# A scan and a segmented attention in one kernel: a new memory plan, crossbar transposes, row-wise attention outputs and big weights as the stationary operand

## The chip, the cores and the metric

The kernel runs on one core of one Trainium2 chip. The metric is the device time of one execution in microseconds (us), lower is better; the kernel before takes 1421 us. Times are medians of several executions.

Names: PE is TensorE (matmul), PEld its weight loads, DVE is VectorE, ACT is ScalarE, POOL is GpSimd, SP is SyncE, which here mostly issues DMAs. SBUF is the on-chip memory, PSUM the matmul accumulators, HBM the memory off the core. Of a matmul's two operands, one is loaded first and stays (the stationary one, loaded by PEld), the other streams past it (the moving one). "Crossbar" stands for DMAs that transpose on the way (DMA_TRANSPOSE in the traces); `xbar` in the code is something else, the mean of B's x.

## The reference, cut to what matters

Two independent halves are computed and set side by side in the output.

```python
# A: a complex diagonal scan. L = 2048 rows, 1024 channels in, 1024 states
Lam_bar = exp(dt * Lam);  Bu = x @ B_bar.T              # complex: two real matmuls
for t in range(L):
    h = Lam_bar * h + Bu[:, t]                           # the scan
y = 2.0 * real(hseq @ Cmat.T) + x * Dskip

# B: 64 segments of 32 rows, 8 memory rows before each; 32 heads of 128
mem = mem0
for s in range(64):
    h = concat([mem, x[:, 32*s : 32*s+32]])              # 40 rows
    q, k, v = h @ Wq, h @ Wk, h @ Wv
    p = softmax(where(mask, q @ k.T * 128**-0.5, -1e9))
    o = (p @ v) @ Wo
    mem = o[:, :8]                                       # next segment's memory
    outs.append(o[:, 8:])
out = concat([y, concat(outs)], axis=-1)                 # bf16, 2048 x 2048
```

B looks serial, because each segment needs the memory rows of the one before. Both kernels **guess** these rows (mean of the segment's 40 rows, with the unknown memory rows taken as zero, times Wv, times Wo), run all segments at once, **check** at the end that the computed memory agrees with the guess, and would fall back on a serial loop if it did not.

## The kernel before: the parts that matter here

Four stages follow each other. (1) *Scan stage*: A's input matmuls and scan, with B's value projection between them. (2) *Scan output and guess*. (3) *Attention*, with the q and k projections between its units. (4) *Out-projection and check*.

Inputs arrive row by row and are needed with the contraction dimension on the partitions, so PE transposes them through PSUM, 128 columns at a time. This is A's x; B's x, and A's input and output weights, are done alike:

```python
        for t in range(4 * tb, 4 * tb + 4):
            xn = self.stg.tile([128, D], BF16, name="a_stg")
            k.SP.dma_start(xn[:], self.x[0][t * 128:(t + 1) * 128, :])
            pt = k.ps("P", (128, 1024), BF16)
            for c in range(KC):
                k.PE.transpose(pt[:, c * 128:(c + 1) * 128], xn[:, c * 128:(c + 1) * 128], k.ident[:])
            k.copy("s" if t % 2 else "v", self.xT[:, :, t * 128:(t + 1) * 128], ...)
```

The scan states go to HBM at the end of every scan unit and come back in the next stage:

```python
        k.SP.dma_start(self.hs[tb][:, pc, :, :], h[:])          # stage1, 32 times
        ...
        hl = pool.tile([128, PC, 2, TB], BF16, name="a_hl", bufs=2)
        k.SP.dma_start(hl[:], self.hs[tb][:])                   # stage2, 4 times
```

An attention unit covers two groups of 99 rows (three segments each) of two heads. Scores stand with the keys on the partitions, so the sum over keys is a matmul with ones; ACT makes its reciprocal as exp(-ln):

```python
        PE.matmul(sm[:, 0:W4], k.ones[0:GW, :], mf, start=True, stop=True)      # 396 wide
        k.S.activation(ln[:], sm[:, 0:W4], ACT.Ln)
        k.S.activation(r[:]..., ln[:], ACT.Exp, scale=-1.0, accum_out=...)
        for gg in range(2):
            for hh in range(2):
                PE.matmul(o[:, gg, hh, :], vt[:, 2 * u + gg, hh * 128:(hh + 1) * 128], m[:, gg, hh, :], ...)
        V.tensor_tensor(ot[...], o[:, :, :, 0:GX], r[:, :, :, 0:GX], ALU.mult)
```

The guess (`og`, then `guess`) has a small stationary operand of 64 or 73 columns and streams the 512-wide weights past it. Its results then stand the wrong way round and are transposed. The check works the same way.

```python
        for c in range(KC):                                                     # og
            k.PE.matmul(p[0:NSEG, :], self.xbar[:, c, :], w[:, c, :], ...)
        ... copy, 4 transposes, copy
```

At the start of the attention stage the program does this:

```python
            wo0 = t32.tile([128, H, 512], BF16, name="t32")
            b.load_wqk(0)
            b.v_mem(0)                                # value rows of the memory, needs 1 MB of Wv
            ...
            k.SP.dma_start(wo0[:], b.Wo[:, :, 0:512]) # 4 MB, first needed in the last stage
```

Of the kernel before, what the change touches and what calls it, by code (L numbers as in the profile page):

```python
# [38 lines left out]
XE = T + NM  # L39

# [6 lines left out]
class K:  # L47
    def __init__(self, tc, ctx):
        self.tc, self.nc = tc, tc.nc
        nc = tc.nc  # L50
        self.V, self.G, self.S, self.PE, self.SP = nc.vector, nc.gpsimd, nc.scalar, nc.tensor, nc.sync
        self.cst = ctx.enter_context(tc.tile_pool(name="cst", bufs=1, side="left"))
        self.psp = ctx.enter_context(tc.tile_pool(name="ps", bufs=1, space=PSUM))
        self.drp = ctx.enter_context(tc.tile_pool(name="dr", bufs=1, space=DRAM))

    def ps(self, tag, shape=(128, 512), dt=FP32):
        return self.psp.tile(list(shape), dt, name="ps" + tag, bufs={"P": 3, "S": 2, "R": 1, "O": 2}[tag])
# [8 lines left out]
def consts(k):  # L66
# [6 lines left out]
    k.ones = c.tile([128, 128], BF16, name="ones")  # L73
    V.memset(k.ones[:], 1.0)

    k.segs = c.tile([128, 4], BF16, name="segs")
    V.memset(k.segs[:], 0.0)
    for j in range(4):
        V.memset(k.segs[32 * j:32 * j + 32, j:j + 1], 1.0)
    k.hpb = c.tile([128, 1], FP32, name="hpb")  # L80
    V.memset(k.hpb[:], HALF_PI)

# [42 lines left out]

class PartA:
    def __init__(self, k, x, Lre, Lim, Bre, Bim, Cre, Cim, logdt, Dskip, out):
        self.k = k
        self.x, self.Lre, self.Lim, self.Bre, self.Bim = x, Lre, Lim, Bre, Bim
        self.Cre, self.Cim, self.logdt, self.Dskip, self.out = Cre, Cim, logdt, Dskip, out  # L130
        self.hs = [k.drp.tile([128, PC, 2, TB], BF16, name=f"a_hs{i}") for i in range(NB)]

    def params(self, pool, tmp):
        k = self.k; V, S, PE, nc = k.V, k.S, k.PE, k.nc
        r24 = tmp.tile([3 * PC, 128], BF16, name="a_r24")
        for i, src in enumerate((self.Lre, self.Lim, self.logdt)):
            nc.scalar.dma_start(r24[i * PC:(i + 1) * PC, :], src.rearrange("(c p) -> c p", p=128))
        pr = k.ps("R")
        PE.matmul(pr[:, 0:3 * PC], r24[:], k.ident[0:3 * PC, 0:3 * PC], start=True, stop=True)
        raw = pool.tile([128, 3, PC], FP32, name="a_raw")  # L140
# [3 lines left out]
        def small(name):  # L144
            return pool.tile([128, PC], FP32, name=name)
        dtb = pool.tile([128, PC], BF16, name="a_dtb")
# [28 lines left out]
        self.rr, self.turn, self.bre, self.bim = rr, turn, bre, bim  # L175
        self.jf = pool.tile([128, TB + 1], FP32, name="a_jf")
        ji = tmp.tile([128, TB + 1], I32, name="a_k1")
# [24 lines left out]

    def load_x(self, tb):
        k = self.k
        for t in range(4 * tb, 4 * tb + 4):
            xn = self.stg.tile([128, D], BF16, name="a_stg")
            k.SP.dma_start(xn[:], self.x[0][t * 128:(t + 1) * 128, :])
            pt = k.ps("P", (128, 1024), BF16)
            for c in range(KC):
                k.PE.transpose(pt[:, c * 128:(c + 1) * 128], xn[:, c * 128:(c + 1) * 128], k.ident[:])  # L210
            k.copy("s" if t % 2 else "v", self.xT[:, :, t * 128:(t + 1) * 128], pt[:].rearrange("p (c n) -> p c n", c=KC))

    def load_b(self, pc):
        k = self.k
        self.bt = self.btp.tile([128, 2, KC, 128], BF16, name="a_bt")
        for i, w in enumerate((self.Bre, self.Bim)):
            wn = self.stg.tile([128, D], BF16, name="a_stg")
            k.SP.dma_start(wn[:], w[pc * 128:(pc + 1) * 128, :])
            pt = k.ps("R", (128, 1024), BF16)
            for c in range(KC):  # L220
                k.PE.transpose(pt[:, c * 128:(c + 1) * 128], wn[:, c * 128:(c + 1) * 128], k.ident[:])
            k.copy("s", self.bt[:, i, :, :].rearrange("p c n -> p (c n)"), pt[:])

    def load_c(self, blk):

        k = self.k
        for i, w in enumerate((self.Cre, self.Cim)):
            wn = self.stg.tile([128, D], BF16, name="a_stg")
            k.SP.dma_start(wn[:], w[blk * 128:(blk + 1) * 128, :])
            pt = k.ps("R", (128, 1024), BF16)  # L230
            for c in range(PC):
                k.PE.transpose(pt[:, c * 128:(c + 1) * 128], wn[:, c * 128:(c + 1) * 128], k.ident[:])
            k.S.activation(self.CT[:, i, :, blk * 128:(blk + 1) * 128], pt[:].rearrange("p (c n) -> p c n", c=PC),
                           ACT.Copy, scale=(-1.0 if i == 1 else 1.0))

    def stage1(self, pc, tb):
# [4 lines left out]
        ur = k.ps("S"); ui = k.ps("O")  # L241
        for i, u in enumerate((ur, ui)):
            for c in range(KC):
                PE.matmul(u[:], self.bt[:, i, c, :], self.xT[:, c, tb * TB:(tb + 1) * TB], start=(c == 0), stop=(c == KC - 1))  # L244
# [3 lines left out]
        V.tensor_tensor(wr[:], ur[:], c_, ALU.mult)  # L248
        V.tensor_tensor(ta[:], ui[:], s_, ALU.mult)
        V.tensor_tensor(wr[:], wr[:], ta[:], ALU.add)  # L250
        V.tensor_tensor(wi[:], ui[:], c_, ALU.mult)
        V.tensor_tensor(ta[:], ur[:], s_, ALU.mult)
# [15 lines left out]
        h = self.wp.tile([128, 2, TB], BF16, name="a_h")  # L268
# [3 lines left out]
        V.tensor_tensor(h[:, 0, :], n1[:], n2[:], ALU.subtract)  # L272
        V.tensor_tensor(n1[:], gr[:], ts2[:], ALU.mult)
        V.tensor_tensor(n2[:], gi[:], tc2[:], ALU.mult)
        V.tensor_tensor(h[:, 1, :], n1[:], n2[:], ALU.add)
        k.SP.dma_start(self.hs[tb][:, pc, :, :], h[:])

    def stage2(self, pool):

        k = self.k; V, G, PE = k.V, k.G, k.PE  # L280
        dB = pool.tile([128, D], BF16, name="a_dB")
        k.SP.dma_start(dB[:], self.Dskip.unsqueeze(0).to_broadcast([128, D]))
        for tb in range(NB):
            hl = pool.tile([128, PC, 2, TB], BF16, name="a_hl", bufs=2)
            k.SP.dma_start(hl[:], self.hs[tb][:])
            for tt in range(4):
                t0 = tb * TB + tt * 128
                xn = pool.tile([128, D], BF16, name="a_xn2", bufs=2)
                k.SP.dma_start(xn[:], self.x[0][t0:t0 + 128, :])
                xd = pool.tile([128, D], FP32, name="a_xd", bufs=2)  # L290
                G.tensor_tensor(xd[:], xn[:], dB[:], ALU.mult)
                ot = pool.tile([128, D], BF16, name="a_ot", bufs=2)
                for half in range(2):
                    hs = slice(half * 512, (half + 1) * 512)
                    py = k.ps("O")
                    for pc in range(PC):
                        for i in range(2):
                            PE.matmul(py[:], hl[:, pc, i, tt * 128:(tt + 1) * 128], self.CT[:, i, pc, hs],  # L298
                                      start=(pc == 0 and i == 0), stop=(pc == PC - 1 and i == 1))
                    V.tensor_tensor(ot[:, hs], py[:], xd[:, hs], ALU.add)  # L300
                    yield
                k.SP.dma_start(self.out[0, t0:t0 + 128, 0:D], ot[:])



class PartB:
    def __init__(self, k, x, mem0, Wq, Wk, Wv, Wo, out):
# [6 lines left out]
        self.os = [k.drp.tile([128, 8, T], BF16, name=f"b_os{i}") for i in range(4)]  # L314
        c = k.cst
        self.m0T = c.tile([128, KC, M], BF16, name="b_m0T")
        self.omT = c.tile([128, H, NM], BF16, name="b_omT")
        self.gm = c.tile([NM, D], FP32, name="b_gm")
# [3 lines left out]
        self.accR = c.tile([128, HP * NU], FP32, name="b_accR")  # L322
# [3 lines left out]
    def init(self, tmp):  # L326
        k = self.k
        k.V.memset(self.accE[:], 0.0)
        m0 = tmp.tile([M, D], BF16, name="b_m0", bufs=1)
        k.nc.scalar.dma_start(m0[:], self.mem0[0])  # L330
        pm = k.ps("R")
        for c in range(KC):
            k.PE.matmul(pm[:, c * M:(c + 1) * M], m0[:, c * 128:(c + 1) * 128], k.ident[0:M, 0:M], start=True, stop=True)
# [4 lines left out]
        z = tmp.tile([32, 512], BF16, name="b_zero", bufs=1)  # L338
        k.V.memset(z[:], 0.0)
        for hb in range(HB):  # L340
            k.G.dma_start(self.vx[hb][64 + NMX:GX, :], z[0:GX - 64 - NMX, :])
            k.G.dma_start(self.vx[hb][T + 32:NSLOT, :], z[0:32, :])

    def load_x(self, t):
        k = self.k
        if t == 0:
            self.pbar = k.ps("P")
        pbar = self.pbar
        xn = self.stg.tile([128, D], BF16, name="b_stg", bufs=3)
        k.nc.scalar.dma_start(xn[:], self.x[0][t * 128:(t + 1) * 128, :])  # L350
        pt = k.ps("P", (128, 1024), BF16)
        for c in range(KC):
            k.PE.transpose(pt[:, c * 128:(c + 1) * 128], xn[:, c * 128:(c + 1) * 128], k.ident[:])
            k.PE.matmul(pbar[:, c * NSEG + 4 * t:c * NSEG + 4 * t + 4], xn[:, c * 128:(c + 1) * 128], k.segs[:], start=True, stop=True)
        ptv = pt[:].rearrange("p (c n) -> p c n", c=KC)
        if t == 0 or t == TT - 1:
            a = XMAIN if t == 0 else t * 128 - 64
            k.copy("s", self.xe[:, :, a:a + 64], ptv[:, :, 0:64])
            b = 0 if t == 0 else T - 64
            k.copy("s", self.xe[:, :, b:b + 64], ptv[:, :, 64:128])  # L360
        else:
            k.copy("s", self.xe[:, :, t * 128 - 64:t * 128 + 64], ptv)

    def fin_xbar(self, tmp):
        k = self.k
        pb = self.pbar[:].rearrange("p (c s) -> p c s", c=KC)
        ms = tmp.tile([128, KC], FP32, name="b_ms", bufs=1)
# [577 lines left out]
```

## Time and profile before

| stage | from, to (us) | PE busy | what limits it |
|---|---|---|---|
| scan stage | 0 to 433 | 395 us | PE; waits for x at the start |
| scan output and guess | 433 to 571 | 129 us | PE |
| hole | 571 to 592 | 0.3 us | a weight load |
| attention | 592 to 1158 | 566 us | PE |
| drain | 1158 to 1176 | 9 us | ACT for the last units, then a wait for the out-projection's input |
| out-projection, check | 1176 to 1420 | 236 us | PE |

The first lines are from the page of the kernel before: busy time by engine, then 40 equal slices of the span, each digit a busy share in tenths.

```profile
span 1420.3 us, 20776 instructions
PE 1335.1 (94%) x8087; PEld 697.2 (49%) x8162; DVE 665.4 (47%) x1495; ACT 488.7 (34%) x1203; POOL 208.0 (15%) x283
...
PE   4889999999997999499999999999999988999998
DMA  5343333243328631943434343433333236213000
...
HBM read 112.50 MB, written 49.30 MB: 114 GB/s over the span
```

PE is the bound nearly everywhere. Next are the same engines' busy times by stretch. The columns are: stretch, its length, busy time and count of PE, PEld, DVE, ACT and POOL, then PE's granted clock (1.00 is full), the DMA engines' share and GB/s.

```profile
0.00:35.00 35.00, 16.45 (x156) 11.70 (x159) 18.97 (x62) 16.46 (x24) 19.22 (x87) 1.00 0.57 187
35.00:100.00 65.00, 54.31 (x440) 32.68 (x445) 39.80 (x80) 33.83 (x46) 0.00 (x0) 0.87 0.42 134
100.00:433.00 333.00, 324.02 (x1642) 151.94 (x1674) 266.54 (x509) 141.40 (x226) 0.00 (x0) 1.00 0.33 108
433.00:571.00 138.00, 129.08 (x578) 59.08 (x589) 24.94 (x41) 3.01 (x4) 33.95 (x16) 0.96 0.51 183
571.00:592.00 21.00, 0.27 (x1) 0.14 (x1) 0.93 (x13) 0.00 (x0) 0.00 (x0) 0.56 1.04 337
592.00:1158.00 566.00, 566.00 (x4137) 328.68 (x4136) 292.38 (x740) 268.41 (x835) 147.25 (x171) 1.00 0.35 100
1158.00:1176.00 18.00, 8.60 (x76) 5.20 (x75) 8.04 (x27) 13.28 (x46) 7.54 (x10) 0.66 1.03 329
1176.00:1420.00 244.00, 236.36 (x1067) 107.81 (x1087) 13.84 (x27) 12.37 (x24) 0.00 (x0) 0.98 0.22 71
```

In attention PE is busy in every microsecond of 566, while DVE and ACT are near half. PE stands still in the hole, for half of the drain, and for 29 us of the first 100. PE's waits, longest first (what waited, for whom: us in total, times, longest):

```profile
PE psP L451 <- DMA b_wv<-in_B_Wv_dram: 21.2, 1, 21.2
PE psP L210 <- DMA a_stg<-in_A_x_dram: 18.2, 6, 9.8
PE psP L615 <- DMA b_ol<-b_os_96: 5.4, 1, 5.4
...
PE psO L298 <- DMA a_hl<-a_hs_76: 3.7, 1, 3.7
PE psS L428 <- DMA b_wog<-in_B_Wo_dram: 3.3, 1, 3.3
```

Two groups of instructions of an attention unit, the sum matmul and the logarithm that follows (busy us in all, mean ns of one, idle time before). The matmul's mean is its whole passage; one follows the other after 0.167 us in a stream:

```profile
L546 PE MATMUL psR<-b_m,ones 99*128 99x396 bf16 x176 | 59.4, 337 | 3.9 <-POOL b_m L537 3.0 <-ACT b_ln L550 0.8
...
L550 ACT ACTIVATE b_ln<-psR 128x396 f32<-128x396 f32 x176 | 87.1, 495 | 0.0
```

### The profile page before, as it was taken

What the parts mean: (1) busy time and instruction counts of PE and PEld (TensorE: products, weight loads), DVE (VectorE), ACT (ScalarE), POOL (GpSimd) and SP (SyncE); (2) the same over time, 40 slices, a digit from 0 to 9 for tenths busy, and PEclk for the clock granted to TensorE, in tenths of its full rate; (3) what the DMA queues carried; (4) which work ended last, traced back from release to release, by engine and by line L of the source; (5) the groups of instructions that cost most, each with busy time, mean ns of one, the idle gap of its engine ahead of it and who ended that gap; (6) DMA issues with size and microseconds to landing.
All of it is one profiled execution on the core that took longest, in us unless ns stands there. A gap on an engine that the chain in (4) does not pass through costs nothing. (4 is left out here: it accounts for less than half of the span.)

```text
span 1420.3 us, 20776 instructions
## 1 busy us (share of the span) xinstructions
PE 1335.1 (94%) x8087; PEld 697.2 (49%) x8162; DVE 665.4 (47%) x1495; ACT 488.7 (34%) x1203; POOL 208.0 (15%) x283
## 2 busy tenths in 40 slices
PE   4889999999997999499999999999999988999998
PEld 3454444444443444255555555555555543444443
DVE  5648988787681122145555555555555550001000
ACT  4453444444431000024444444444444460000000
POOL 5000000000001222012222222222222230000000
PEclk9899999999998999699999999999999988999999
DMA  5343333243328631943434343433333236213000
GB/s 185 127 133 112 104 104 111 97 136 117 112 82 299 246 129 60 292 110 92 123 92 124 92 123 92 124 92 94 92 94 92 61 126 208 94 55 111 23 16 24
DMA packets 159742, 163.20 MB, mean 115 GB/s; under 512 B 9152, under 2 KB 132656, under 8 KB 159128
## 3 DMA queue, kind: packets, MB, share of 16 engines
q1 hardware_dynamic: 156760, 157.13, 35.2%
q10 hardware_dynamic: 2368, 4.22, 0.9%
q8 instruction: 66, 1.08, 0.3%
q0 software_dynamic: 512, 0.47, 0.1%
q14 instruction: 36, 0.29, 0.1%
HBM read 112.50 MB, written 49.30 MB: 114 GB/s over the span
## 5 line engine op out<-in xcount | busy, mean ns | idle before, releaser
L388 PE MATMUL psP<-b_wv,b_xe 128*128 128x512 bf16 x1006 | 228.2, 381 | 1.1
L507 PE MATMUL psP<-b_xe,b_wk 128*128 128x480 bf16 x1024 | 225.8, 365 | 0.0
L507 PE MATMUL psP<-b_xe,b_wq 128*128 128x480 bf16 x1024 | 223.4, 365 | 0.0
L534 ACT ACTIVATE b_e<-psS 99x396 bf16<-99x396 f32 x176 | 88.5, 503 | 374.5 <-PE psS L531 370.8
L537 POOL TENSOR_TENSOR b_m<-b_e,maskB 99x396 bf16<-99x396 bf16 x160 | 139.8, 873 | 348.8 <-ACT b_e L534 348.8
L557 DVE TENSOR_TENSOR b_ot<-psO,b_r 128x384 bf16<-128x384 f32 x176 | 98.2, 558 | 192.0 <-ACT b_r L551 178.8
L388 PEld LDWEIGHTS <-b_xe 128*128 128x128 bf16 x1024 | 99.9, 98 | 118.3 <-issue 2.4
L615 PEld LDWEIGHTS <-b_ol 128*128 128x128 bf16 x896 | 88.1, 99 | 112.9 <-DMA b_ol<-b_os_96 5.2
L507 PEld LDWEIGHTS <-b_wq 128*128 128x128 bf16 x1024 | 95.7, 97 | 93.7
L507 PEld LDWEIGHTS <-b_wk 128*128 128x128 bf16 x1024 | 95.4, 97 | 92.6
L298 PE MATMUL psO<-t_111,a_hl 128*128 128x512 bf16 x500 | 114.0, 386 | 4.4 <-DMA a_hl<-a_hs_76 3.7
L61 ACT ACTIVATE b_vst<-psP 128x512 bf16<-128x512 f32 x128 | 75.4, 589 | 95.9 <-PE psP L388 90.0
L615 PE MATMUL psP<-t_5172,b_ol 128*128 128x512 bf16 x438 | 101.5, 386 | 5.8 <-DMA b_ol<-b_os_96 5.4
L63 DVE CAST b_ost<-psP 128x512 bf16<-128x512 f32 x16 | 11.1, 692 | 200.3 <-PE psP L615 200.3
L615 PE MATMUL psP<-wo_12598,b_ol 128*128 128x512 bf16 x438 | 98.9, 379 | 0.5
L551 ACT ACTIVATE b_r<-b_ln 128x396 f32<-128x396 f32 x176 | 94.2, 535 | 5.4
L550 ACT ACTIVATE b_ln<-psR 128x396 f32<-128x396 f32 x176 | 87.1, 495 | 0.0
L61 ACT ACTIVATE b_ost<-psP 128x512 bf16<-128x512 f32 x16 | 9.6, 597 | 218.1 <-PE psP L615 204.9
L298 PEld LDWEIGHTS <-a_hl 128*128 128x128 bf16 x512 | 50.7, 99 | 66.2 <-DMA a_hl<-a_hs_76 4.2
L244 PEld LDWEIGHTS <-a_bt 128*128 128x128 bf16 x512 | 48.7, 99 | 55.7 <-issue 5.3
L300 DVE TENSOR_TENSOR a_ot<-psO,a_xd 128x512 bf16<-128x512 f32 x32 | 22.1, 692 | 110.8 <-PE psO L298 87.5
L244 PE MATMUL psS<-a_xT,a_bt 128*128 128x512 bf16 x242 | 63.8, 391 | 1.4 <-issue 1.0
(492 smaller groups left out, 1568.9 us busy)
## 6 DMA issues: line engine op xcount, KB each, us to landing
b_wv<-in_B_Wv_dram SPq DMA_DIRECT2D x16, 1024.0 KB
b_wog<-in_B_Wo_dram SPq DMA_DIRECT2D x8, 1024.0 KB
b_wq<-in_B_Wq_dram SPq DMA_DIRECT2D x16, 512.0 KB
b_wk<-in_B_Wk_dram SPq DMA_DIRECT2D x16, 512.0 KB
a_stg<-in_A_x_dram SPq DMA_DIRECT2D x16, 256.0 KB
b_stg<-in_B_x_dram ACTq DMA_DIRECT2D x16, 256.0 KB
out_dram<-a_ot SPq DMA_DIRECT2D x16, 256.0 KB
t_5172<-in_B_Wo_dram SPq DMA_DIRECT2D x1, 4096.0 KB
```

Source lines behind the costliest of these rows:

```text
L61: self.S.activation(out, in_, ACT.Copy)
L244: PE.matmul(u[:], self.bt[:, i, c, :], self.xT[:, c, tb * TB:(tb + 1) * TB], start=(c == 0), stop=(c == KC - 1))
L298: PE.matmul(py[:], hl[:, pc, i, tt * 128:(tt + 1) * 128], self.CT[:, i, pc, hs], start=(pc == 0 and i == 0), stop=(pc == PC - 1 and i == 1))
L300: V.tensor_tensor(ot[:, hs], py[:], xd[:, hs], ALU.add)
L388: k.PE.matmul(p[:], self.xe[:, c, t * 128:(t + 1) * 128], w[:, c, :], start=(c == 0), stop=(c == KC - 1))
L507: PE.matmul(p[:, 0:480], w[i][:, c, hh * 128:(hh + 1) * 128], self.xe[:, c, 480 * q:480 * q + 480], start=(c == 0), stop=(c == KC - 1))
L534: k.S.activation(e[:], s[0:GW], ACT.Exp, scale=float(E) ** -0.5, accum_out=self.accE[0:GW, i:i + 1])
L537: k.G.tensor_tensor(m[:], e[:], mask[0:GW, :, :].unsqueeze(2).to_broadcast([GW, 2, 2, GW]), ALU.mult)
L550: k.S.activation(ln[:], sm[:, 0:W4], ACT.Ln)
L551: k.S.activation(r[:].rearrange("p a b q -> p (a b q)"), ln[:], ACT.Exp, scale=-1.0, accum_out=self.accR[:, i:i + 1])
L557: V.tensor_tensor(ot[:, :, 2 * u * GX:(2 * u + 2) * GX].rearrange("p h (g n) -> p g h n", n=GX), o[:, :, :, 0:GX], r[:, :, :, 0:GX], ALU.mult)
L615: PE.matmul(p[:], lhs, self.wo[half][:, h, :], start=(h == 0), stop=(h == H - 1))
```

## The change

The intent is a new memory plan. Scan states stay in SBUF, which leaves out their way through HBM. Transposing loads go through the DMA crossbar, and PE and PSUM are spared. Attention outputs are made row-wise (queries on the partitions), so that the softmax sum is one more column of the value matmul. Guess and check take the big weights as the stationary operand. Six rotating 8 KB-per-partition buffers hold most of the weights, so the next stage's weights can be loaded ahead. Part of the out-projection is moved up to fill the drain. The core of a long diff, with cuts:

```diff
 def load_x(self, tb):                                          # A; B's x, B_re/B_im and C alike
-            xn = self.stg.tile([128, D], BF16, name="a_stg")
-            k.SP.dma_start(xn[:], self.x[0][t * 128:(t + 1) * 128, :])
-            ... 8 PE transposes and a copy
+        self.xT[tb] = k.w8((KC, TB), "xT")
+        k.SP.dma_start(self.xT[tb], self.x[0][tb * TB:(tb + 1) * TB, :], transpose=True)
 ...
-        k.SP.dma_start(self.hs[tb][:, pc, :, :], h[:])
+            self.hs[tb] = self.hsp.tile([128, PC, 2, TB], BF16, name="a_hs", bufs=4)
 ...
 def og(self, hb, w):
-        for c in range(KC):
-            k.PE.matmul(p[0:NSEG, :], self.xbar[:, c, :], w[:, c, :], ...)
-        ... copy, 4 transposes
+        for h in range(4):
+            for c in range(KC):
+                k.PE.matmul(p[:, h * NSEG:(h + 1) * NSEG], w[:, c, h * 128:(h + 1) * 128], self.xbar[:, c, :], ...)
 ...
 def att_back(self, hp, u, m):
-        PE.matmul(sm[:, 0:W4], k.ones[0:GW, :], mf, start=True, stop=True)
-        k.S.activation(ln[:], sm[:, 0:W4], ACT.Ln)
-        k.S.activation(r[:]..., ln[:], ACT.Exp, scale=-1.0, accum_out=...)
-                PE.matmul(o[:, gg, hh, :], vt[:, 2 * u + gg, hh * 128:(hh + 1) * 128], m[:, gg, hh, :], ...)
+                cs = slice(hh * 129, hh * 129 + 129)               # 128 values and a column of ones
+                PE.matmul(o[:, gg, cs], m[:, j * GW:j * GW + 128], vt[:, 2 * u + gg, cs], start=True, stop=True)
+        V.reciprocal(r..., ends)                                    # 99 x 4
+        V.tensor_tensor(ot..., oa[:, :, 1:257]..., r...to_broadcast([GW, 2, 2, E]), ALU.mult)
+            k.SP.dma_start(os[64:64 + 20 * GX, cs]..., ot[0:GX, 1:21, :])   # to HBM, rows of 512 B
 ...
 def load_o(self, tb, q):                                       # and back, transposed
+        k.SP.dma_start(t[:], self.os[q][tb * 512:(tb + 1) * 512, :], transpose=True)
 ...
-            k.SP.dma_start(wo0[:], b.Wo[:, :, 0:512])
+                if u == 4 and 8 <= hp < 12:
+                    w = k.w8((8, 512), "wo0")
+                    k.SP.dma_start(w, b.Wo[:, 8 * (hp - 8):8 * (hp - 7), 0:512])
+                if done == want:
+                    next(early, None)                               # out-projection ahead
```

## The prediction

> **What bounds the kernel now.** TensorE: the page shows PE busy 94% of 1420.3 us. Spacing in the timeline: a 128x512 matmul every 0.216 us in a stream, a 480-wide one every 0.203, a 99-wide one every 0.044, the 396-wide ones matmul 0.167. In the busy-time-by-stretch view: scan stage to 433 us, scan output and guess to 571, attention with projections 592 to 1158, its drain to 1176, out-projection to the end. DVE is 75 to 85% busy in the scan stage, under 55% in attention; the DMA engines about a third. PE falls short in five places: the first 100 us (29 us idle, clock 0.87 from 35 to 100, waits on x loads); 433 to 450 (10 us idle); 571 to 592 (21.2 us for b_wv, the longest wait); 1158 to 1176 (about 15 us: last units without projections, then 5.4 us for b_ol); the last 7 us.
>
> **What the change does.**
> 1. Crossbar DMA transposes replace 512 PE transposes (8 in 0.44 to 0.6 us) and 128 segment-sum matmuls: about -36 us of PE in the scan stage, and their ACT and DVE copies. DVE gains five segment sums (about 4 us each, estimated from 0.69 us per 512 elements).
> 2. Scan states stay in SBUF: 16.8 MB of DMA and the 3.7 us wait for a_hl vanish. Mostly off the critical path.
> 3. Attention: values become the moving operand (129 wide with a ones column), so the 396-wide sum matmul, Ln and second Exp go. Per unit PE loses 0.167 us and gains 4 x 0.013: -0.12 us x 176 = -20 us, in a PE-bound stage. ACT's cut (495 + 535 + 189 ns per unit) is off the path, except in the drain.
> 4. Stationary weights in guess, og and check: each time 64 512-wide matmuls (13.8 us) become 256 of 64 to 73. At 0.05 to 0.06 us (estimated from the transposes' spacing), 13 to 15 us: nothing won but dropped transposes and copies.
> 5. The next stage's weights are loaded ahead through six rotating buffers: the 21.2 us wait should go, and most of the 433 us gap.
> 6. Out-projection work (48 matmuls in attention, 144 right after) fills the drain: about -12 us.
> Attention outputs go to HBM in 512 B pieces and come back through the crossbar, 16 MB; hidden if it is quick.
>
> **Sum (us).** Scan stage 346 of PE + 9 first load + 20 start-up, cold clock and DVE stalls = 375; scan output and guess 127 (502); attention 566 - 20 + 10 moved in + 5 boundary = 561 (1063); tail 211 + check 14 + stalls 6 + end 7 = 238. About 1301; plus 5 for crossbar loads at the start: 1306 us, 8% less. Range 1265 to 1365.
>
> **Uncertain: crossbar speed.** No trace here has it. The Trainium skill ("Advanced Engine Details and Errata", X-Bar Transpose) says trn2 transposes run about as fast as ordinary DMA; before moved 187 GB/s in the first 35 us. The new start wants 8 MB transposed in about 65 us, 125 GB/s, plus weights. At 100 GB/s or below the start loses 25 us or more, the tail (5 MB wanted right after attention) some 15.
>
> **Signs.** Right: scan stage ends near 375; no wait over 5 us on b_wv; attention near 33.5 us per head pair with PE near 100%; no hole before the out-projection. Wrong: PE waits on b_xe, xT or b_ol transposes; PE below 95% in the scan stage because DVE (over 90%) holds psO; attention slowed by two instead of three psP buffers, or by late b_v.
>
> **What would make it wrong.** Slow crossbar DMAs, or in-order SP issue behind a blocked DMA.
>
> Chances: faster by over 2% 0.92, within 2% 0.04, slower 0.04.

## The result, and the profile after

The changed kernel takes **1281.13 us** (median of four, 1279.19 to 1283.15), the kernel before 1421.03 us (four, 1419.6 to 1422.62). The ratio is 0.9018, with a 95% interval of 0.8999 to 0.9036: 9.8% less time. Ratios here and below are from runs of the same rounds; they are not quite the ratios of the medians quoted.

The page of the changed kernel:

```profile
span 1277.1 us, 19342 instructions
PE 1236.8 (97%) x7815; PEld 650.2 (51%) x7885; DVE 630.8 (49%) x1330; ACT 320.2 (25%) x746; POOL 213.3 (17%) x307
...
PE   6698999999999999999999999999999999999997
...
HBM read 72.65 MB, written 43.66 MB: 91 GB/s over the span
```

PE lost 98 us of work and 45 us of idle time (span less PE busy: 85.2 before, 40.3 after). Its busy times by stretch, with the same columns as before:

```profile
0.00:35.00 35.00, 19.55 (x88) 8.42 (x90) 17.99 (x36) 7.13 (x12) 22.55 (x91) 1.00 1.03 207
35.00:100.00 65.00, 57.76 (x256) 25.94 (x261) 61.51 (x121) 26.39 (x46) 0.00 (x0) 0.92 0.56 140
100.00:372.00 272.00, 266.13 (x1428) 124.78 (x1452) 238.30 (x456) 99.95 (x176) 0.00 (x0) 0.99 0.34 98
372.00:492.00 120.00, 117.45 (x756) 57.67 (x769) 36.70 (x64) 3.80 (x5) 37.36 (x40) 1.00 0.57 176
492.00:1052.00 560.00, 559.44 (x4089) 330.30 (x4091) 257.77 (x620) 171.94 (x488) 153.34 (x176) 1.00 0.59 121
1052.00:1277.00 225.00, 216.43 (x1205) 103.11 (x1224) 18.50 (x37) 10.96 (x19) 0.00 (x0) 0.99 0.39 88
```

| stage | before (us) | predicted | after |
|---|---|---|---|
| scan stage | 433 | 375 | 371.8 |
| scan output and guess, with the hole | 159 | 127 | 120.0 |
| attention | 566 | 561 | 560.0 |
| drain, out-projection, check | 262 | 238 | 225.3 |

The last attention units count to the drain before and to attention after.

Attention is still PE without a gap; it lost the sum matmuls and took in out-projection work. The hole and the drain are gone. The two longest waits that PE has left lie at the start, where the DMA engines are now full (share 1.03); the third ends at 113 us, the fourth lies in the scan output stage:

```profile
PE psO L262 <- DMA w<-in_A_x_dram: 11.5, 1, 11.5
PE psP L402 <- DMA b_xe<-in_B_x_dram: 10.9, 1, 10.9
PE psS L402 <- DMA w<-in_B_Wv_dram: 4.5, 1, 4.5
PE psS L316 <- DVE a_ot L318: 1.8, 1, 1.8
```

### The profile page after: what moved, and what is told of

It reads as the page before. It is cut to its first block, busy times and chain, and to the rows that moved or that the text cites. A ratio compares the mean times of both kernels' runs of the same rounds, so it can differ in the third digit from the quotient of the medians.

```text
span 1277.1 us, 19342 instructions
## 1 busy us (share of the span) xinstructions
PE 1236.8 (97%) x7815; PEld 650.2 (51%) x7885; DVE 630.8 (49%) x1330; ACT 320.2 (25%) x746; POOL 213.3 (17%) x307
## 3 DMA queue, kind: packets, MB, share of 16 engines
q8 instruction: 63, 1.03, 0.3%
## 5 line engine op out<-in xcount | busy, mean ns | idle before, releaser
L522 PE MATMUL psP<-b_xe,w 128*128 128x480 bf16 x2048 | 439.6, 366 | 0.0
L522 PEld LDWEIGHTS <-w 128*128 128x128 bf16 x2048 | 194.2, 98 | 185.2
L77 DVE CAST b_q<-psP 128x480 bf16<-128x480 f32 (+1 forms) x192 | 98.1, 532 | 151.1 <-PE psP L522 139.6
L402 PEld LDWEIGHTS <-b_xe 128*128 128x128 bf16 x1024 | 100.8, 99 | 138.9 <-DMA b_xe<-in_B_x_dram 10.9
L622 PEld LDWEIGHTS <-b_ol 128*128 128x128 bf16 x1024 | 99.5, 98 | 117.5
L75 ACT ACTIVATE b_k<-psP 128x480 bf16<-128x480 f32 x128 | 73.3, 572 | 306.2 <-PE psP L522 306.2
L402 PE MATMUL psP<-w,b_xe 128*128 128x512 bf16 x509 | 122.4, 382 | 11.0 <-DMA b_xe<-in_B_x_dram 10.9
L262 PE MATMUL psO<-w,a_bt 128*128 128x512 bf16 x487 | 115.9, 383 | 12.8 <-DMA w<-in_A_x_dram 11.5
L402 PE MATMUL psS<-w,b_xe 128*128 128x512 bf16 x508 | 123.2, 385 | 4.8 <-DMA w<-in_B_Wv_dram 4.5
L573 DVE TENSOR_TENSOR b_ot<-psO,b_rall 99x512 bf16<-99x512 f32 x176 | 121.6, 691 | 6.4
L622 PE MATMUL psO<-b_xe,b_ol 128*128 128x512 bf16 x500 | 112.2, 379 | 0.6
L622 PE MATMUL psO<-w,b_ol 128*128 128x512 bf16 x376 | 84.4, 379 | 0.4
```

The source lines that it names most:

```text
L75: self.S.activation(out, in_, ACT.Copy)
L77: self.V.tensor_copy(out, in_)
L262: PE.matmul(u[:, i, :], self.bt[:, i, c, :], self.xT[tb][:, c, :], start=(c == 0), stop=(c == KC - 1))
L402: k.PE.matmul(p[:], self.xe[:, c, t * 128:(t + 1) * 128], w[:, c, :], start=(c == 0), stop=(c == KC - 1))
L522: PE.matmul(p[:, 0:480], w[:, i * KC + c, hh * 128:(hh + 1) * 128], self.xe[:, c, 480 * q:480 * q + 480], start=(c == 0), stop=(c == KC - 1))
L573: V.tensor_tensor(ot[:, 2 * u:2 * u + 2, :].rearrange("p g (h e) -> p g h e", h=2), oa[:, :, 1:257].rearrange("p g (h e) -> p g h e", h=2) ...
```

## The experiments

Twelve kernels ran, five rounds each. All were correct but one. Kernels named `b_` start from the kernel before, `e_` from the changed one. The changed kernel itself gave ratios of 0.9018 and 0.9035 in two batches. Across batches a difference below about 2.5 us (0.0017 of 1420) is therefore not resolved. Differences in us below are differences of medians.

### The yardstick: the changed kernel again

> The changed kernel once more, unchanged, as the yardstick of this chip for the other three: 1279 to 1284 us, as before.

Measured: 1281.07 us (1280.1 to 1281.56), ratio 0.9035 (0.9021 to 0.9048). The first two experiments ran in this batch, on the same chip.

### Attention: was it PE's sum matmul or ACT's work?

The change takes both from each of 176 units. One run gives PE its 396 columns back, as two 198-wide matmuls into unused PSUM columns that nobody reads. The other gives ACT its Ln and Exp back, unread.

```diff
 # e_sum
+        for gg in range(2):
+            PE.matmul(o[:, gg, 258:456], k.ones[0:GW, :], m[:, 198 * gg:198 * gg + 198], start=True, stop=True)
 # e_act
+        k.S.activation(ln[:], e[:], ACT.Ln)
+        k.S.activation(rr[:], ln[:], ACT.Exp, scale=-1.0)
```

> The changed kernel with the row-sum matmul put back: two 198-wide matmuls of the all-ones tile per attention unit into unused PSUM columns, nobody reads them, no other engine gets work. Theory (attention is bound by TensorE alone, so 396 columns per unit are worth their streaming time): 176 x 0.167 = +29 us, about 1310 us, and PE still near 100% busy in attention. Rival (the attention stage got shorter because ScalarE was relieved of Ln and Exp, or because other waits went): under +5 us.

Measured: 1310.3 us (1309.16 to 1312.42), ratio 0.9245 (0.9229 to 0.9261), or 29.2 us more; 176 times the 0.167 us read from the trace is 29.4.

> The changed kernel with the Ln and the second Exp of 99x396 put back on ScalarE in every attention unit, results unused: about 176 x 1.0 us = 180 us more of ScalarE work. Theory (ScalarE is off the critical path while projections feed TensorE): +0 to +4 us, the little being in the last units; about 1283 us. Rival (ScalarE's relief is what shortened attention): +20 us or more.

Measured: 1282.49 us (1281.25 to 1283.29), ratio 0.9042 (0.9028 to 0.9056), or 1.4 us more, which is not resolved. The same stretch of attention in the changed kernel, with e_sum and then e_act after it:

```profile
500.00:1040.00 540.00, 539.95 (x3953) 319.57 (x3952) 247.42 (x586) 166.26 (x470) 146.53 (x168) 1.00 0.58 116
```

```profile
500.00:1040.00 540.00, 540.00 (x4069) 331.34 (x4068) 236.42 (x560) 157.23 (x444) 137.67 (x158) 1.00 0.55 111
```

```profile
500.00:1040.00 540.00, 539.95 (x3941) 319.20 (x3941) 246.65 (x584) 338.81 (x803) 145.03 (x167) 1.00 0.58 115
```

ACT's busy time doubles (166.26 to 338.81 us) and the time stays. The stage is bound by PE and not by ACT; more work for DVE or POOL was not tried.

### The drain

The out-projection matmuls that the change spreads over the last units are moved behind attention. It was not enough to move them in the program: the scheduler hoisted them again (the author's account), so they are pinned in program order.

```diff
-                if done == want:
-                    next(early, None)
+            mm = k.PE.matmul(self.acc[t, half], ...)
+            if self.pin and h8 == 0:
+                k.tc.keep_in_program_order(mm)
```

> The changed kernel with the early out-projection matmuls (48 inside the last attention units, 144 after) pinned behind all of attention, so the last 13 units run with nothing to fill TensorE. Theory: those units then go at the pace of POOL, about 0.9 us each (11.7 us) where TensorE needs 0.41, so about +6 us: 1287 us, with TensorE idle about 6 us near 1035 to 1046. Rival (the filling is worth the whole 15 us hole of the kernel before): +12 us or more; other rival (nothing): under +2.

Measured: 1288.3 us (1287.99 to 1288.92), ratio 0.9086 (0.9073 to 0.91), or 7.2 us more, so the filling is worth 7 us in the new kernel, not the 12 or more of the rival. What set the pace of the last units stands in the traces. First the kernel before, then e_nodrain, with the columns of the other stretches:

```profile
1158.00:1170.00 12.00, 7.98 (x72) 4.67 (x70) 6.27 (x21) 11.94 (x42) 7.54 (x10) 0.75 0.99 319
```

```profile
1037.00:1046.00 9.00, 5.66 (x74) 4.07 (x74) 7.70 (x21) 5.55 (x20) 9.00 (x11) 1.00 1.04 338
```

In the kernel before ACT is busy for 11.94 of 12 us, and the units follow each other every 1.38 us. In e_nodrain, without Ln and Exp (495 and 535 ns per unit in the kernel before), POOL is the full engine (9.00 of 9), and the units follow every 0.83 us, near the 0.9 of the theory. The 5.4 us wait for `b_ol` at the end of the drain is also gone in e_nodrain, although nothing fills there: its load comes earlier in the new plan. So there was less of a drain left to fill.

### Which operand stands still

`og` and `guess` are turned back to the small stationary operand with 512-wide moving weights, with their transposes and copies. The check is left as changed.

```diff
 # e_moving, og; guess alike
-        for h in range(4):
-            for c in range(KC):
-                k.PE.matmul(p[:, h * NSEG:(h + 1) * NSEG], w[:, c, h * 128:(h + 1) * 128], self.xbar[:, c, :], ...)
+        for c in range(KC):
+            k.PE.matmul(p[0:NSEG, :], self.xbar[:, c, :], w[:, c, :], ...)
+        ... copy, 4 transposes, copy
```

> The changed kernel with the guess and the eight value-mean products (og) turned back: weights move (512 wide, 64 matmuls each), the 64-column matrix is stationary, then PE transposes and copies. Theory from the trace of the change (32 stationary-weight matmuls of 64 columns take 0.93 us, 29 ns each, not the 50 to 60 ns of the prediction, against 8 moving ones in 1.73 us): +6.4 us for each of the two, and about 2 to 4 us for the transposes and their waits, so +15 to +17 us, about 1297 us. Rival (the prediction's size: equal cost): +2 to +4 us.

Measured: 1294.56 us (1294.13 to 1294.88), ratio 0.9121 (0.9103 to 0.9138), or 13.5 us more. One eighth of the guess in the timeline of the changed kernel (start, length, engine, line, tiles, count), and of e_moving:

```profile
404.23 1.10 PE L434 MATMUL psO<-b_ogT,w 128*128 128x64 bf16 x32
405.16 1.03 PE L316 MATMUL psS<-w,a_hs 128*128 128x512 bf16 x3
```

```profile
404.28 1.91 PE L437 MATMUL psO<-w,b_ogT 128*64 128x512 bf16 x8
406.12 3.63 PE L316 MATMUL psS<-w,a_hs 128*128 128x512 bf16 x15
```

The next group starts 0.93 us after 32 64-wide matmuls, 29 ns each, and 1.84 us after eight 512-wide ones. Each of the 32 needs a weight load of its own, recorded as 98 ns; but the 256 loads of the guess take only 8.6 us of PEld's busy time, so they overlap, and they do not show in the spacing. So the stationary form halves PE's work here, where I had taken the two for equal.

### Scan states through HBM

The new kernel also writes its states to HBM and reads them back, 16.8 MB in all, without using what it reads. A second run writes only.

```diff
 # e_hsdram; e_hswrite has the first addition alone
+        k.SP.dma_start(self.hsd[tb][:, pc, :, :], h[:, pc, :, :])
 # stage2
+                    if tt == 0 and half == 0:
+                        hl = pool.tile([128, PC, 2, TB], BF16, name="x_hl", bufs=1)
+                        k.SP.dma_start(hl[:], self.hsd[tb][:])
```

> The changed kernel, which also writes each scan state to HBM and reads all four blocks back into an unused tile, 16.8 MB more DMA as in the kernel before; the matmuls still read the copy in SBUF. Theory (the round trip was off the critical path): +0 to +4 us, the little from the DMA-bound first 50 us. Rival (keeping the states in SBUF is a large part of the gain): +10 us or more.

Measured: 1295.66 us (1294.36 to 1299.2), ratio 0.9136 (0.9116 to 0.9155), or 14.6 us more. My theory, that it costs 0 to 4 us, fell.

> The changed kernel, which also writes each scan state to HBM (8.4 MB) but reads nothing back. In the run that did both, the scan stage grew by about 1 us and the scan-output stage by about 12 us. Theory (the writes hide in the scan stage, and the reads are what hurts, by crowding the scan-output stage's weight and x loads): +0 to +3 us, 1281 to 1284 us. Rival (the writes hurt too, for instance by waiting on VectorE in the in-order SP queue ahead of other loads): +5 us or more.

Measured: 1283.94 us (1279.45 to 1285.39), ratio 0.9048 (0.9023 to 0.9072). That is 2.9 us more, and hardly resolved. So adding the reading costs about 12 us. PE's waits in e_hsdram that the changed kernel does not have or has shorter:

```profile
PE psO L439 <- DMA w<-in_B_Wo_dram: 5.9, 4, 3.7
PE psS L321 <- DVE a_ot L323: 5.4, 1, 5.4
```

In the scan output stage of e_hsdram (372 to 505 us) PE does 120.5 us of work in 133, at a DMA share of 0.72 and a clock of 0.96; in the changed kernel 117.5 in 120, at 0.57 and 1.00. The states' return shares the DMA engines with the guess's 8 MB of Wo and with x for A's skip term. But it also shares SP's queue: there, from 365 to 450 us, SP stood 38.2 us before writes of `a_ot`, against 23.5 us in the changed kernel, with later loads behind them. How much is bandwidth and how much the order of one queue was not separated. And part of the 5.4 us wait comes with the writes: e_hswrite has 3.6 us of it, the changed kernel 1.8. One more caution belongs here: this read-back comes all in the first half of the stage and has one buffer. In the kernel before it had two buffers and was spread, and PE waited 3.7 us for it and 3.3 us for Wo. What it cost there is less than 12 us by these waits, but was not isolated.

### Transposing in the crossbar, in the kernel before

Only A's x and A's input weights come transposed by DMA; this replaces 256 of the 512 PE transposes.

```diff
-        ... 4 loads, 32 transposes, 4 copies
+        k.SP.dma_start(self.xT[:, :, tb * TB:(tb + 1) * TB], self.x[0][tb * TB:(tb + 1) * TB, :], transpose=True)
-            ... load, 8 transposes, copy
+            k.SP.dma_start(self.bt[:, i, :, :], w[pc * 128:(pc + 1) * 128, :], transpose=True)
```

> The kernel before with crossbar transposes for A's x and B alone (256 of its 512 PE transposes go, with their PSUM copies). Theory (each PE transpose costs TensorE about 0.055 us in a PE-bound stage): -14 us of TensorE time, and -5 to -15 us of start waits on these loads, so -19 to -29 us, 1390 to 1400 us. Rival (the crossbar is so slow that its waits eat the gain): -5 us or less, with waits of TensorE on a_xT or a_bt.

Measured: 1393.92 us (1390.69 to 1397.46), ratio 0.9822 (0.9799 to 0.9845), or 25.4 us less. The crossbar pays in the old memory plan too. The other half (B's x, with its segment sums, and C) was not undone by itself.

### Transposed or plain loads at the start, in the changed kernel

A's x and input weights come as plain loads of the same bytes. Half A is then wrong on purpose (relative error 0.073); the work is the same.

```diff
-        k.SP.dma_start(self.xT[tb], self.x[0][...], transpose=True)
+        k.SP.dma_start(self.xT[tb].rearrange("p a b -> p (a b)"), self.x[0][...].rearrange("(p r) d -> p (r d)", p=128))
```

> The changed kernel with part A's x and B loaded by ordinary DMA instead of the crossbar: same bytes, same tiles, not transposed, so A's half of the result is wrong on purpose. The start of the changed kernel moves 207 GB/s at a DMA share of 1.03, so it is DMA-bound. Theory (a crossbar transpose takes more DMA time per byte than an ordinary load, which reached about 290 GB/s elsewhere in these traces): 2.5 of the 7.5 MB needed by 42 us get cheaper by a third, so TensorE's 11.5 us wait on A's x shrinks by 4 to 8 us and the whole by as much, 1273 to 1277 us. Rival (the crossbar is as fast as an ordinary load): within 1 us of 1281.

Measured: 1278.39 us (1277.13 to 1280.18), ratio 0.9013 (0.8992 to 0.9035). That is 2.7 us less; the interval takes in both ratios of the changed kernel, so it is not resolved, and it is less than the 4 to 8 us that the theory gave. PE's wait for A's x sinks from 11.5 to 8.7 us, which agrees. The issue of a 1 MB transposing load took SP 4.0 to 6.0 us in the changed kernel; a plain one took 0.43 to 0.58 us here. Most of the wait for A's x is therefore not due to its own transposing. B's x still came transposed, and PE still waited 10.7 us for it, so what transposing costs the start as a whole is not shown.

### The hole of 21 us, in the kernel before

The 4 MB load of the first half of Wo is split into four and issued in head pairs 8 to 11, as the change does. The pieces too are pinned.

```diff
-            k.SP.dma_start(wo0[:], b.Wo[:, :, 0:512])
+                if u == 4 and 8 <= hp < 12:
+                    tc.keep_in_program_order(k.SP.dma_start(wo0[:, 8 * (hp - 8):8 * (hp - 7), :], ...))
```

> The kernel before with its 4 MB load of the first half of Wo moved from the start of attention to four 1 MB pieces at head pairs 8 to 11. Theory (the 21.2 us hole at 571 us is queueing: the three weight loads that TensorE needs stand behind 4 MB at about 290 GB/s, 14 us): -12 to -14 us, 1405 us, with a wait of 7 to 9 us left for loads that can't be issued before their memory is free. Rival (the hole is the time from the release of the pool to the landing of the loads whatever stands before them): 0 to -4 us.

Measured: 1409.45 us (1408.91 to 1410.79, six runs), ratio 0.9932 (0.9914 to 0.9949), or 9.9 us less: more than the rival, less than the theory. SP's queue at the hole in the kernel before shows the mechanism:

```profile
570.61 0.39 SPq L851 DMA_DIRECT2D t_5172<-in_B_Wo_dram  x1
571.39 8.08 SPq L302 DMA_DIRECT2D out_dram<-a_ot  x1
579.53 0.42 SPq L477 DMA_DIRECT2D b_wq<-in_B_Wq_dram  x1
580.00 2.87 SPq L477 DMA_DIRECT2D b_wk<-in_B_Wk_dram  x1
582.91 2.96 SPq L375 DMA_DIRECT2D b_wv<-in_B_Wv_dram  x1
```

The scheduler put the 4 MB first, though the program has it last. The next issue took 8.08 us, and the urgent Wv was issued 12.3 us after the bulk load. In b_wo0late the wait for it is still there, at half the length:

```profile
PE psP L451 <- DMA b_wv<-in_B_Wv_dram: 10.2, 1, 10.2
```

So about half of the hole was the queue behind 4 MB. The other half remains when the load moves; these loads are still issued only at 570.8 us, right after the stage's last output writes. In the changed kernel both halves are gone; what the rotating buffers alone do was not isolated.

### A try at a better start, which failed

In the first 113 us of the changed kernel PE waits 27 us for loads (11.5, 10.9 and 4.5). The second megabyte of Wv is loaded early, so that 16 instead of 8 value tiles can fill the time; A's second block, the segment sums and `og` move with it.

```diff
+            wv1 = b.load_wv(1)                      # before A's first loads
-            while done < 8:
+            while done < 16:
                 next(v); done += 1
```

> A try at a faster kernel: the changed kernel with the second 1 MB of Wv loaded before A's x, so that the eight x tiles that are there serve two weight blocks (13.8 us of matmuls for 1 MB loaded, against 6.9 for 1 MB of x); the segment sums come before the first scan units, where VectorE is idle; the value-mean product og is allowed from the third unit on, so that its weight buffer frees earlier. Theory (the 11.5 us wait at 30 us and the 4.5 us wait at 108 us, with some 3 us of half-clock matmuls after them, are all there is to gain): -10 to -16 us, 1265 to 1271 us. Rival (VectorE, 95% busy from 35 to 100 us, is the real limit of the scan stage, so waits only move): within 4 us of 1281, with TensorE waiting for psO instead.

Measured: 1290.1 us (1288.65 to 1290.92), ratio 0.9095 (0.9075 to 0.9116), or 9.0 us **more**; no theory had that. The longest new wait:

```profile
PE psS L404 <- ACT b_vst L75: 18.6, 1, 18.6
ACT b_vst L75 <- DMA b_vx<-b_vst: 17.7, 5, 8.4
```

PE waited for ACT to empty a PSUM tile, ACT for a staging buffer, and that for its write to HBM. The first of these writes was issued only at 41.4 us, although the first tiles had been copied at 15 us: eight transposing loads were issued between, from the one queue of SP.

This wait is not the whole of the loss, though. By 140 us PE had done only 1.7 us less work than in the changed kernel (110.91 against 112.60), since the waits of 11.5 and 4.5 us had gone. Most of the loss came where the scan stage ends (the changed kernel, then e_wv1):

```profile
360.00:402.00 42.00, 39.92 (x293) 20.25 (x296) 28.20 (x53) 7.18 (x11) 9.15 (x8) 1.00 0.75 214
```

```profile
360.00:402.00 42.00, 32.17 (x245) 16.59 (x247) 35.99 (x71) 6.32 (x9) 3.36 (x3) 0.89 0.78 221
```

That is 7.7 us. Sixteen value tiles had been done ahead at the old pace, so they ran out before the last scan units, and PE then waited for Wo (4.8 us) and for DVE (4.7 us).

### The same, with the writes on another queue

The writes of the first 16 value tiles go to ACT's DMA queue. A's second block is loaded before B's last quarter, and the pacing is adjusted.

```diff
-            k.SP.dma_start(vx[s0:s0 + n * 128, :]..., st[:, 0:n, :])
+            (k.nc.scalar if hb < 2 else k.SP).dma_start(vx[s0:s0 + n * 128, :]..., st[:, 0:n, :])
-            for t in range(2, 4):
-                b.load_x(t * 512, t * 512 + 512)
+            b.load_x(1024, 1536)
             a.load_x(1)
+            b.load_x(1536, 2048)
```

> The changed kernel with its start rearranged again: as in the last try the second block of B's value weights (1 MB) is loaded early and 16 instead of 8 value units run before the scan, but now (1) the writes of the first 16 value tiles are issued on ScalarE's DMA queue, so that they do not stand in line behind the transposing loads on SyncE's, (2) A's second 512 rows are loaded before the last quarter of B's x, (3) the value units between scan units are paced at 3.75 instead of 4 per scan unit, and the short sums over B's x are placed later. Theory (PE's start is lost to the 18.6 us wait for the value staging, which was a queueing effect): that wait falls under 4 us, the first 50 us hold about 8 to 12 us more PE work than the changed kernel's (27.5 us of 50), and the time is 1281 - 8 to - 14 = 1267 to 1273 us. Rival (the first 50 us are bound by the DMA engines, share above 1.0 at 207 to 240 GB/s, so that a wait removed is only moved to the next load, and the early megabyte pushes A's loads back): within 4 us of 1281, or slower, with PE busy in 0:50 no more than 32 us and a new wait for a load.

Measured: **1272.96 us** (1272.56 to 1276.37), ratio 0.8959 (0.8946 to 0.8972). This beats both kernels, by 8 us against the changed one; the ratio's interval lies clear of 0.9035 (0.9021 to 0.9048). The stretch from 0 to 50 us in the changed kernel and in e_best (in e_wv1 PE was busy for 21.38 us of it):

```profile
0.00:50.00 50.00, 27.52 (x117) 11.66 (x119) 31.71 (x59) 12.18 (x22) 22.55 (x91) 0.90 1.03 219
```

```profile
0.00:50.00 50.00, 31.45 (x124) 12.88 (x127) 21.13 (x51) 15.99 (x28) 22.26 (x91) 0.93 1.10 217
```

And PE's waits for the staging in e_best:

```profile
PE psS L407 <- ACT b_vst L76: 5.1, 2, 4.7
PE psP L407 <- ACT b_vst L76: 1.4, 1, 1.4
```

The wait of 18.6 us is down to 6.5, and the first write is issued at 19.3 us instead of 41.4: that fits the queue as its cause, though loads and sums were moved in the same run. Against e_wv1 PE gained 7.1 us of work by 140 us, and another 7.2 us from 360 to 402 us (39.38 against 32.17), where it is the new pacing that fits. The time came where the theory had it, but the signs did not fully: the wait should have been under 4 us and PE's work in the first 50 us higher by 8 to 12, and it is higher by 3.9 (31.45 less 27.52). The rival had allowed it no more than 32, so it is right on that sign. By 140 us the gain in PE's work is 5.4 (118.00 against 112.60). The profiled execution was also the slowest of the five. Where the remaining microseconds come from is open.

## Why the prediction was right, and which of its steps were not

The time, 1281 us, lies within the range 1265 to 1365, 25 us below the predicted 1306; the class, faster by over 2%, is right. Point by point:

1. **Transposes leave PE: right.** About 36 us of PE work were predicted for all of them, segment sums included. Half of the transposes gave 25.4 us in the old kernel: PE's busy time fell by 20.2 us (14 were expected) and its idle time by 7.9. The whole was not undone by itself.
2. **Scan states "mostly off the critical path": wrong for the changed kernel, open for the kernel before.** Written and read back they cost the changed kernel 14.6 us. The writes (2.9 us) nearly hide, in a stage with a DMA share of 0.34. The read-back (about 12 us) does not; its stage already moves 176 GB/s at a share of 0.57 and loads 8 MB of weights just in time. An average DMA share of a third over the span did not tell this.
3. **Attention -20 us, ACT off the path: right.** Giving the matmul back costs 29.2 us; less the 4 x 0.013 us per unit that the wider value matmuls add (9 us), that is the 20 predicted. ACT's work costs nothing that can be resolved (1.4 us). The stage took 560.0 us; 561 was predicted.
4. **Stationary weights "nothing won": wrong by size.** The step that failed is the estimate of 0.05 to 0.06 us per 64- to 73-wide matmul, taken from the spacing of 128-wide transposes. Measured: 29 ns for 64 columns (0.93 us for 32). For 73 columns it is about 34 ns: 64 of them in the check took 2.16 us. Each of the three sets of 256 costs 7.4 to 8.6 us instead of 13 to 15. Undoing two of the three cost 13.5 us, with their transposes and copies.
5. **The 21.2 us wait: right that it goes.** Half of it was the 4 MB queued ahead, half stayed when only that load was moved.
6. **The drain, -12 us: direction right, size off.** In the changed kernel the filling is worth 7.2 us, since the drain itself has become shorter: the units follow every 0.83 us instead of 1.38.
7. **Crossbar speed, the named uncertainty: near the good end.** The start moved 207 GB/s at a DMA share of 1.03; 125 plus weights had been asked for. The Trainium skill ("Advanced Engine Details and Errata", X-Bar Transpose), on which the prediction leaned, has transposes as fast as ordinary DMA, at 350 to 400 GB/s. The trace does not show that rate: in the changed kernel's scan output stage (400 to 450 us), with plain loads, 250 GB/s took a share of only 0.81. The lower figure of 261 GB/s for a less regular pattern in "DMA: Bandwidth & Descriptors" (Latency and other measured facts) is nearer. Whether it is the transposing that holds the start to 207 GB/s is not separated: with A's inputs loaded plainly it moved 212 GB/s at 1.02, and the 2.7 us saved are not resolved. PE does wait for the crossbar's data at the start, 22.4 us in two waits, but the prediction had allowed 29 us for the start (9 and 20), and PE's idle time up to 372 us came to 28.6.

The sum was 1301 us and 5 for the crossbar. The span came out at 1277.1: the scan stage 3.2 lower, scan output and guess 7.0 lower, attention 1.0 lower, the tail 12.7 lower, and the 5 were not needed. Point 4 accounts for about 5 to 7 us in each of the three stages with guess and check work. In the scan stage part of that went elsewhere; where is not resolved. In the tail some 4 us more are stalls that were allowed for and did not come: PE is idle 8.6 of 225 us, where 13 had been set aside. The rest of the tail's 12.7 is open.

What single runs or waits account for adds up to some 87 of the 140 us (25.4, 20, 13.5, 7.2 and the 21.2 us hole). They come from two different kernels, so this sum is a rough estimate. The rest, above all the transposes of B's x and of C, the segment sums and the check, was not undone by itself.

## What to carry to other kernels

Cost a small matmul by its own measured spacing, not by that of a wider one: making the big matrix stationary halved PE's work here, with 64 columns on the moving side. Before calling a transfer hidden, look at the DMA share and at the just-in-time loads of the stage where it lands, reads above all; an average over the span says nothing about that. And look at the order in which one queue really issues: a bulk load or a row of slow transposing loads ahead of a small urgent transfer stood behind waits of 21 and 19 us here, and after either was moved half or less was left. Then look at PE's work stretch by stretch, since the longest wait need not be where the time was lost.

## What the Trainium skill lacked or had wrong

- "Advanced Engine Details and Errata", X-Bar Transpose: transposing loads as fast as regular ones, 350 to 400 GB/s. Here a start dominated by them moved 207 to 219 GB/s at a DMA share of 1.03, mixed with some plain loads, and plain transfers moved 250 GB/s at 0.81. With A's inputs loaded plainly the start still moved only 212 GB/s at 1.02, so the runs do not show that rate, but do not refute it either.
- No page that I read gives, for this chip, the time that a transposing load of a megabyte holds its issuing queue: 4.0 to 6.0 us on SP at the start, against 0.43 to 0.58 us for a plain megabyte. A quarter of a megabyte with nothing ahead of it took 1.37 us. Other issues can be long too: 8.08 us for an output write behind the 4 MB in the kernel before. Eight of them, large and small, held up a small write for some 25 us.
- "TensorE: Matmul & The Clock Gate", Back-to-back issue gap: for streams of weight load and matmul it gives about 81 ns per matmul at 128 columns and 131 ns at 512. Here such pairs took 29 ns at 64 columns, about 34 ns at 73 and 216 ns at 512 (16 in 3.46 us); 129-wide ones in attention took 58 ns (4 in 0.23 us). The isolated figures on the same page (a floor of about 25 ns at 64 columns and below, 518 cycles of 2.4 GHz at 512) nearly fit these streams; those for the streams do not. The prediction would have been nearer with the floor.
- "DMA: Bandwidth & Descriptors", Queues, rings and completion order: SP and ACT each own a row of the queues, and an engine takes turns between rows. The page adds (Issuing engines are not separate DMA queues) that issuing from several engines saves only the issue time, usually small beside the transfer. Here it was not small: eight transposing issues held SP from 15.8 to 41.3 us, and with the writes on ACT's row, and a few other moves, a wait of 18.6 us became 6.5 us.
